# A long-convolution filter and a gated MLP on one core: the filter's sums and differences formed by TensorE, a third buffer for its values, and the second step's loads issued with the first

## The chip, the cores and the metric

One NeuronCore of a Trainium2 chip runs the kernel. The metric is the device time of one execution in microseconds (us). The engines are named as the profile names them: PE is TensorE (PEld its weight loads), DVE is VectorE, ACT is ScalarE, POOL is GpSimd, and SP issues the DMAs.

## The reference

Four batches of 12480 positions with 128 channels are convolved along the positions with a filter that a small network makes, gated, and sent through an MLP. Everything is float32.

```python
h_mlp  = np.maximum(pos_emb @ w1, 0.0) @ w2          # 12480x64 @ 64x64, @ 64x128
h_filt = h_mlp * np.exp(-0.01 * pos)[:, None]
u = x * v
y = irfft(rfft(u, n=2*S) * rfft(h_filt, n=2*S))[:, :S, :]
z = (x * y).reshape(B * S, D)                          # 49920 x 128
h = z @ moe_w_in                                       # 128 -> 2048
out = (h * np.cos(h)) @ moe_w_out                      # 2048 -> 128
```

## The kernel before, in words

**The convolution** is a Fourier transform in two steps, done as matmuls with tables of cosines and sines. A position is n = n1 * 120 + n2 with n1 below 104 and n2 below 120. The first step (`f1_units`, matmul on L402) works along n1 into 96 frequencies, the second (`f2_units`, L442) along n2; then comes the product with the filter's spectrum (`f2_product`, L458 to L461) and two steps back (`i1_units`, L466, and `i2_units`, L491). Of every two opposite n2 (n2 and 119 - n2) the kernel keeps a sum and a difference, so that the second step needs half the table for each.

**The filter** is made first. `filter_load` brings eleven pieces of `pos_emb`; `filter_scale` multiplies them on DVE by the decaying window (which commutes with the ReLU, being positive); `filter_turn` transposes them on PE; `filter_hidden` (L341 to L346) multiplies by `w1` and lets ACT write the ReLU into `aT`. Two positions lie on the partitions of one tile: 64 hidden values of an even n2 on the lower half and of the odd n2 after it on the upper half. `w1_sb` and `w2_sb` are therefore block-diagonal. `filter_out` (L348 to L361) takes a pair of n2 and the pair opposite to it: two matmuls of 256 columns give four positions, ACT copies two of them to `above`, and DVE makes one sum and one difference from PSUM and `above` (L359), straight into `ftile`. There are 30 such calls.

**The signal.** `u_units` loads x and v by groups of four n2 (two tiles of 208 KB; three buffers for x, two for v), multiplies the two halves (`u_multiply`, L390, each half on the engine that a small function names), and makes sums on POOL and differences on DVE (`u_sums`, L396). For batch 0 it runs beside the filter, as the generator `first_u`; the loops that make the filter call `next(first_u)` a written number of times: twice an iteration from the fifth on in the hidden layer, 40 times in all in the 30 calls of `filter_out`, and then once for every two units of the filter's first step.

**The order of all this is written out by hand.** The schedule is manual: each engine runs its instructions in the order in which the program records them, and SP issues the DMAs in that order too. A DMA that has to wait holds up what stands behind it in SP's order. The stages of the first 345 us are: the hidden layer; `filter_out` with the signal; the filter's first step (`f1_evict_filter`, L424 to L435, each unit on ACT or on DVE by a share of 0.53) with the rest of the signal; the end of that step beside `inverse_tables`, which makes ten tables with POOL's arithmetic and ACT's Sin (`Tables.sines`; the Sin of a table is recorded `lag` tables later); the first step for batch 0 beside the conversion of `moe_w_in` from float64; `f2_both_units`, in which the second step of the signal and that of the filter share the table `w` that DVE and ACT make (L289, L291); and the first step back.

In `f2_both_units` the filter's values of two frequencies go from PSUM to a tile `h` (ACT, L614), are stored to DRAM (`hd`, L616) for the other batches, and are used by the product. The pool has two buffers of each tile. `w` is stored to `wd`.

**The long part.** From about 345 us on, the MLP's 98 groups of rows are the main thread (16 pieces each: `moe_up` L725 with a range reduction on ACT, DVE and POOL, `moe_act` L739 and L741, `moe_down` L750), and the convolutions of the batches are a generator `conv` from which a piece is drawn whenever the main thread has gone as many steps as the last piece was worth. `forward_units` is the chain first step, second step, first step back; `f2_units` loads `w` and `h` two iterations ahead from `wd` and `hd` into three buffers each (L581, L583). `moe_store` (L759 to L777) transposes a finished group on PE, copies it to `ob` on ACT (L765) and issues its stores on SP (L773), all at one place of the order, halfway through the pieces of the next group.

Of the kernel before, what the change touches and what calls it, by code (L numbers as in the profile page):

```python
# [9 lines left out]
F32 = mybir.dt.float32  # L10
U32 = mybir.dt.uint32
AF = mybir.ActivationFunctionType
ALU = mybir.AluOpType
# [3 lines left out]
P = 128  # L17
# [13 lines left out]
def kernel(  # L31
# [46 lines left out]
    nc = tc.nc  # L78

    B, S, D = x.shape  # L80
    FO = pos_emb.shape[1]
    DFF = moe_w_in.shape[1]
    N1, N2 = 96, 120
# [167 lines left out]

    def inverse_tables(pool):

        t = Tables(pool, nc.gpsimd, 2)
        part = t.whole([P, 1], [[1, 1]], channel_multiplier=1, name="part")
        part4 = t.whole([P, 1], [[1, 1]], base=1, channel_multiplier=4, name="part4")
        step = t.whole([P, P], [[1, P]], name="step")
        mid = t.whole([P, P], [[1, P]], base=-MID, name="mid")
        cs, rows, tw_t = back_tables(pool)
        yield from t.sines(step, part, N2, [(cs[:, 0, 0:H + 1], 1), (cs[:, 1, 0:H + 1], 0)],  # L260
                           eighths=slice(0, H + 1, H))
        yield from t.sines(step[:, 1:H], part, N2,
                           [(cs[:, 0, H + 1:], 0), (cs[:, 1, H + 1:], 1)])
        yield from t.sines(step, part4, 4 * N1,
                           [(rows[:, i, :], q) for i, q in enumerate((0, 1, 2, 3))])
        yield from t.sines(mid, part4, TURN, [(tw_t[:, 0, :], 1), (tw_t[:, 1, :], 0)],
                           eighths=slice(H - 1, N2, H))
        t.finish(1)
        for kept, made in ((csd, cs), (rowsd, rows), (twd, tw_t)):
            nc.sync.dma_start(kept[:, :, :], made[:, :, :])  # L270

# [68 lines left out]

    def filter_hidden(bank, aT, i, peT, w1_sb):  # L341

        pa = bank()
        nc.tensor.matmul(pa[:, 0:ROWS * H], w1_sb[:, :], peT[:, :], start=True, stop=True)
        nc.scalar.activation(aT[:, 0:H, i * ROWS:(i + 1) * ROWS],
                             pa[:, 0:ROWS * H].rearrange("p (n a) -> p a n", a=H), AF.Relu)  # L346

    def filter_out(pool, bank, aT, slots, j, w2_sb):  # L348

        ps = bank()  # L350
        for i, jj in enumerate((j, H - 1 - j)):
            nc.tensor.matmul(ps[0:FR, i * 2 * D:(i + 1) * 2 * D], aT[:, jj, 0:FR],
                             w2_sb[:, :], start=True, stop=True)
        above = pool.tile([FR, 2, CB, 2], F32, name="above", bufs=2)
        pj = ps[0:FR, :].rearrange("p (n b i) -> p n b i", n=4, i=2)
        nc.scalar.copy(out=above[:, :, :, :], in_=pj[:, 2:4])
        a = H - 2 - 2 * j
        for place, op in ((a, ALU.add), (ODD + a, ALU.subtract)):
            nc.vector.tensor_tensor(  # L359
                slots[0:FR, :, place:place + 2, :].transpose([0, 2, 1, 3]),  # L360
                pj[:, 1::-1], above[:, :, :, :], op=op)  # L361

    def n2s(g):

# [229 lines left out]
    def f2_both_units(bank):  # L594

        with tc.tile_pool(name="both", bufs=2) as pool:
            ws = {}

            def before(j):
                ws[j] = pool.tile([KE, 2, N2], F32, name="w")  # L600
                for i in range(2):
                    make_w(ws[j][:, i, :], 2 * j + i, half=bank)
                nc.sync.dma_start(wd[j, :, :, :], ws[j][:, :, :])

            def mm(j, ps, i):
                if i == 0:
                    ps = bank(), bank()
                for filt in range(2):
                    f2_mm(ps[filt], ws[j], 2 * j, i, filt=filt == 1)
                return ps  # L610

            def after(j, ps):
                h = pool.tile([N2, 2, 2, D], F32, name="h")
                nc.scalar.activation(h[:, :, :, :].rearrange("p g r d -> p (g r d)"),  # L614
                                     ps[1][0:N2, :], AF.Copy, scale=1.0 / M)
                nc.sync.dma_start(hd[j, :, :, :, :], h[:, :, :, :])  # L616
                yield from f2_product(pool, ps[0], h, 2 * j)

            yield from units(N1 // 2, F2_STEPS, before, mm, after, 4, ahead=1)
# [69 lines left out]

    def forward_units(bank, back):  # L690

        yield from f1_units(bank, slots[0:R, :, :, :])
        yield from f2_units(bank)
        next(back)
        yield from i1_units(bank)

# [3 lines left out]
    def first_row(n):  # L700
        return min(R + (n - 1) * P, NROWS) if n else 0
# [54 lines left out]
        nc.scalar.copy(out=ot[:, 0:m], in_=accs.pop(n)[:, 0:m])  # L756
        return ot

    def moe_store(pool, n, ot):  # L759
        m = rows_of(n)  # L760
        pt = ps_h.tile([P, BANK], F32, name="ph")
        for i in range(G):
            transpose(pt[0:m, i * D:(i + 1) * D], ot[:, i * m:(i + 1) * m], ident)
        ob = pool.tile([P, 2, UA * D], F32, name="ob", bufs=1)
        nc.scalar.copy(out=ob[0:m, :, :].rearrange("p h n -> p (h n)"), in_=pt[0:m, :])  # L765
        row = first_row(n)
        while row < first_row(n + 1):
            b, g, n1 = row // R // NG, row // R % NG, row % R
            count = min(R - n1, first_row(n + 1) - row)
            first, _, second, _ = n2s(g)  # L770
            start = out[b * S + n1 * N2 + first, :]
            at = row - first_row(n)
            nc.sync.dma_start(  # L773
                bass.AP(tensor=start.tensor, offset=start.offset,
                        ap=[[N2 * D, count], [(second - first) * D, 2], [1, UA * D]]),
                ob[at:at + count, :, :])
            row += count  # L777

    with tc.manual_schedule():
        with tc.tile_pool(name="psum", bufs=8, space=PSUM) as psum, \  # L780
                ExitStack() as first:
            def bank():
                return psum.tile([P, BANK], F32, name="ps")
# [5 lines left out]
            aT = above.rearrange("p b j i -> p b (j i)")  # L789


            keep = first.enter_context(tc.tile_pool(name="keep", bufs=1, side="right"))
            w2_sb = keep.tile([P, 2 * D], F32, name="w2_sb")
            nc.gpsimd.memset(w2_sb[:, :], 0.0)
            with tc.tile_pool(name="layers", bufs=1, side="right") as pool:
                w1_sb = pool.tile([P, P], F32, name="w1_sb")
                nc.gpsimd.memset(w1_sb[:, :], 0.0)
# [1 line left out]
                for m in range(2):  # L799
                    nc.sync.dma_start(  # L800
                        w1_sb[m * FO:(m + 1) * FO, m * FO:(m + 1) * FO], w1[:, :])
                    nc.sync.dma_start(
                        w2_sb[m * FO:(m + 1) * FO, m * D:(m + 1) * D], w2[:, :])
                for i in range(1, NCH):
                    pes[i] = filter_load(pool, i)
                first_u = u_units(0, 3, slots[0:R, :, :, :],
                                  lambda j, half: nc.vector if half and j % 3 and j < 18
                                  else nc.gpsimd)
                next(first_u)
                ident = pool.tile([P, P], F32, name="ident")  # L810
                make_identity(nc, ident)
                window = filter_window(pool)
                nc.gpsimd.memset(aT[:, 0:H, NCH * ROWS:FR], 0.0)
                sines = forward_tables(pool)
                peTs = {}
# [14 lines left out]
            fpool = first.enter_context(tc.tile_pool(name="ftile", bufs=1, side="right"))  # L830
            ftile = fpool.tile([P, CB, N1 + KF, 2], F32, name="ftile")
            clear_gap(ftile[0:FR, :, :, :])
            with tc.tile_pool(name="out", bufs=1, side="right") as pool:
                for j in range(H // 2):
                    filter_out(pool, bank, aT, ftile, j, w2_sb)
                    for _ in range(1 + (j % 3 == 0)):
                        next(first_u)
            f1 = f1_units(bank, ftile[0:FR, :, :, :], 0.53, f1_evict_filter)
            for _ in first_u:
                for _ in range(2):  # L840
                    next(f1)
            with tc.tile_pool(name="tables", bufs=1) as pool:
                sines = inverse_tables(pool)
                for i, _ in enumerate(f1):
                    if i % 5 == 0:
                        next(sines, None)
                for _ in sines:
                    pass
# [60 lines left out]
            next(conv)  # L909
        moe_turn(mpool, 0)  # L910
        steps = [(n, c) for n in range(NALL) for c in range(NFC)]
        hidden, gates, ots = {}, {}, {}
        for i in range(len(steps) + LAG):
            if i < len(steps):
                n, c = steps[i]
# [12 lines left out]
            if i < len(steps):  # L928

                if c == (LAG - 1 if n else NFC - 2) and n + 1 < NALL:  # L930
                    moe_turn(mpool, n + 1)
                if c == NFC // 2 and n - 1 in ots:
                    moe_store(mpool, n - 1, ots.pop(n - 1))
            owed += 1.0
            while owed > 0.0:
                owed -= next(conv, owed)
        for n in sorted(ots):
            moe_store(mpool, n, ots[n])
# [1 line left out]
_INS = ['x', 'v', 'pos_emb', 'w1', 'w2', 'moe_w_in', 'moe_w_out']  # L940
_OUTS = [((49920, 128), 'float32')]
# [25 lines left out]
```

## Time and profile before

| | |
|---|---|
| median of three runs | 3795.7 us (3795.18 to 3796.21) |
| the profiled execution, its own time | 3799.85 us |
| its span, first to last instruction | 3798.0 us |
| mean granted clock of TensorE | 0.991 |
| busy: PE, DVE, POOL, ACT | 3709.6, 2769.4, 2592.8, 2520.0 us |
| DMA | 276 MB, 24.8% of 16 engines |
| 0 to 31.9 us | hidden layer of the filter |
| 31.9 to 64.9 us | `filter_out` beside the signal |
| 64.9 to 96.5 us | filter's first step beside the signal |
| 96.5 to 120.9 us | its end, beside the ten tables |
| 120.9 to 169.8 us | signal's first step, conversion of `moe_w_in` |
| 169.8 to 277.5 us | joint second step |
| 277.5 to 342.8 us | first step back, conversion of `moe_w_out` |
| 342.8 us to the end | MLP with the convolutions beside it |

The profile gives durations in us, for one of an instruction in ns where that is marked; a count after "x" says how many instructions a group holds. A float32 matmul shows as two PE instructions. "Idle before" names what ended an engine's rest. In the table of waits a line is: the waiting engine and line, what it waited for, the total, how often, the longest. A busy share is an average over the stretch; what counts is which engine ends last there.

### The profile page before, as it was taken

Reading aid. Unit: us, or ns where it says so; the run is one execution under the profiler, and the core shown is the slowest. Engines: PE = TensorE matmul, PEld = TensorE weight load, DVE = VectorE, ACT = ScalarE, POOL = GpSimd, SP = SyncE. Lnnn points to the kernel's source line nnn. Section 1 sums busy time; section 2 is a strip of 40 time slices with the busy share of each in tenths; the row PEclk is TensorE's granted clock in tenths of the full one; section 3 lists DMA queues with packets and bytes.
Section 4 is the critical chain, followed back from the end, with each engine's and each line's share of the span. In section 5 each row is a group of like instructions: output and inputs, shape, how many; then the busy total and the mean of one; then the engine's idle time right before and its main releaser. Section 6 shows DMA issues by size and latency. Waiting matters only on the chain.

```text
span 3798.0 us, 47246 instructions
## 1 busy us (share of the span) xinstructions
PE 3709.6 (98%) x13546; PEld 2114.1 (56%) x13546; DVE 2769.4 (73%) x5658; ACT 2520.0 (66%) x4683; POOL 2592.8 (68%) x2342
## 2 busy tenths in 40 slices
PE   7898999999999999999999999999999999999999
PEld 6777555645466555555565556555566544444444
DVE  7887887678876777778766886788765566666666
ACT  5756776756665557766655557666664677777777
POOL 7667886478854665588845664788644577777776
PEclk9899999999999999999999999999999999999999
DMA  6253551022201650122203540222105300000000
GB/s 165 70 177 96 148 152 54 12 76 78 73 27 49 178 172 24 36 76 75 63 16 102 175 129 12 61 78 73 48 12 159 95 17 23 17 17 23 17 21 15
DMA packets 209499, 276.14 MB, mean 73 GB/s; under 512 B 17111, under 2 KB 146535, under 8 KB 209111
## 3 DMA queue, kind: packets, MB, share of 16 engines
q1 hardware_dynamic: 209239, 273.12, 24.8%
q8 instruction: 109, 1.79, 0.2%
q14 instruction: 151, 1.24, 0.1%
HBM read 193.64 MB, written 79.42 MB: 72 GB/s over the span
## 4 chain that ended last, share of the span: by engine, by line
PE 81%; POOL 7%; DVE 4%; DMA 3%; ACT 3%; issue 2%; SPq 0%; POOLq 0%; ACTq 0%; DVEq 0%
PE ph L725 31%; PE acc L750 26%; PE cv L750 5%; PE cv L491 4%; PE cv L466 4%; POOL f L734 4%; PE cv L402 3%; PE cv L442 3%; PE ph L126 2%; DMA hd<-h 1%; PE ps L402 1%; DMA tm<-td 1%; ACT cs L739 1%; DVE k L731 1%; POOL tm L295 1%
## 5 line engine op out<-in xcount | busy, mean ns | idle before, releaser
L734 POOL TENSOR_TENSOR f<-a,k 128x512 f32<-128x512 f32 (+1 forms) x1568 | 1988.7, 1268 | 1062.3 <-DVE k L731 1060.2
L725 PE MATMUL ph<-at,w_in_sb 128*128 128x512 f32 (+1 forms) x3136 | 1601.5, 592 | 5.8 <-DVE gt L741 5.3
L728 ACT ACTIVATE a<-ph,quarter 128x512 f32<-128x512 f32 (+1 forms) x1568 | 1073.4, 685 | 764.8 <-PE ph L725 755.7
L750 PE MATMUL acc<-gt,w_out_sb 128*128 128x512 f32 (+1 forms) x2688 | 1375.2, 593 | 9.7 <-ACT ot L756 9.3
L741 DVE TENSOR_TENSOR gt<-ph,cs 128x512 f32<-128x512 f32 (+1 forms) x1568 | 1077.7, 687 | 319.3 <-ACT cs L739 291.8
L731 DVE TENSOR_SCALAR k<-a 128x512 f32<-128x512 f32 (+1 forms) x1568 | 770.0, 491 | 629.9 <-ACT a L728 608.4
L739 ACT ACTIVATE cs<-f 128x512 f32<-128x512 f32 (+1 forms) x1568 | 980.5, 625 | 334.7 <-POOL f L734 332.4
L750 PEld LDWEIGHTS acc<-gt,w_out_sb 128*128 128x128 f32 x2688 | 506.1, 189 | 663.6 <-issue 620.4
L725 PEld LDWEIGHTS ph<-at,w_in_sb 128*128 128x128 f32 x3136 | 554.5, 190 | 339.5 <-issue 266.8
L461 POOL TENSOR_TENSOR slots<-slots,t 120x256 f32<-120x256 f32 x384 | 311.9, 818 | 63.8 <-DVE t L460 26.9
L491 PEld LDWEIGHTS cv<-slots,tm 96*104 96x104 f32 x1920 | 241.2, 171 | 109.3 <-issue 79.3
L491 PE MATMUL cv<-slots,tm 96*104 96x128 f32 x1920 | 255.5, 275 | 9.1 <-DVE tm L291 4.9
L750 PE MATMUL cv<-gt,w_out_sb 128*128 128x512 f32 (+1 forms) x448 | 224.5, 583 | 0.7 <-DVE gt L741 0.7
L466 PEld LDWEIGHTS cv<-cs,slots 120*96 120x96 f32 x1536 | 176.7, 167 | 67.6 <-issue 65.7
L466 PE MATMUL cv<-cs,slots 120*96 120x120 f32 x1536 | 183.1, 266 | 0.0
L442 PE MATMUL cv<-slots,w 124*120 124x256 f32 x576 | 173.6, 381 | 7.0 <-DMA w<-wd 7.0
L442 PEld LDWEIGHTS cv<-slots,w 124*120 124x120 f32 x576 | 103.8, 184 | 131.0 <-issue 118.1
L402 PEld LDWEIGHTS cv<-c,slots 104*124 104x124 f32 x768 | 132.5, 192 | 71.2 <-issue 58.3
L402 PE MATMUL cv<-c,slots 104*124 104x192 f32 x768 | 151.2, 326 | 4.8 <-DVE gt L741 3.5
L750 PEld LDWEIGHTS cv<-gt,w_out_sb 128*128 128x128 f32 x448 | 84.9, 190 | 104.5 <-issue 99.5
L390 DVE TENSOR_TENSOR xt<-xt,vt 104x256 f32<-104x256 f32 x177 | 138.3, 789 | 0.1
L476 DVE TENSOR_TENSOR slots<-cv,other 96x240 f32<-96x240 f32 x384 | 133.7, 394 | 4.2 <-ACT other L474 4.2
(129 smaller groups left out, 2585.8 us busy)
## 6 DMA issues: line engine op xcount, KB each, us to landing
h<-hd SPq DMA_DIRECT2D x144, 240.0 KB
tm<-td SPq DMA_DIRECT2D x96, 312.0 KB
xt<-in_x_dram SPq DMA_DIRECT2D x120, 208.0 KB
vt<-in_v_dram SPq DMA_DIRECT2D x120, 208.0 KB
xs<-in_x_dram SPq DMA_DIRECT2D x120, 208.0 KB
zd<-zs SPq DMA_DIRECT2D x119, 208.0 KB
zb<-zd SPq DMA_DIRECT2D x96, 256.0 KB
w<-wd SPq DMA_DIRECT2D x144, 116.2 KB
```

The source lines that it names most:

```text
L402: nc.tensor.matmul(ps[0:KE, i * 2 * N1:(i + 1) * 2 * N1], u[:, b, 0:KE, i], c1[0:u.shape[0], :, :].rearrange("p r k -> p (r k)"), start=Tr ...
L442: nc.tensor.matmul(pi, w[:, i, :], parts[0:KE, :, k], start=True, stop=True)
L461: nc.gpsimd.tensor_tensor(y[:, r], y[:, r], t[:, r], op=op)
L466: nc.tensor.matmul(ps[0:N1, (i * 2 + r) * N2:(i * 2 + r + 1) * N2], parts[0:N2, r, :, b, i], cs[:, r, :], start=True, stop=True)
L491: nc.tensor.matmul(ps[0:R, i * D:(i + 1) * D], t[:, i, r, :], slots[0:N1, :, place, :], start=(r == 0), stop=(r == 1))
L725: nc.tensor.matmul(ph[:, 0:m], w_in_sb[:, c * P:(c + 1) * P], ats[n][:, 0:m], start=True, stop=True)
L728: nc.scalar.activation(a[:, 0:m], ph[:, 0:m], AF.Identity, bias=quarter[:, 0:1], scale=INV_TWO_PI)
L731: nc.vector.tensor_scalar(out=k[:, 0:m], in0=a[:, 0:m], scalar1=ROUND, scalar2=ROUND, op0=ALU.add, op1=ALU.subtract)
L734: nc.gpsimd.tensor_tensor(f[:, 0:m], a[:, 0:m], k[:, 0:m], op=ALU.subtract)
L739: nc.scalar.activation(cs[:, 0:m], f[:, 0:m], AF.Sin, scale=TWO_PI)
L741: nc.vector.tensor_tensor(gt[:, 0:m], ph[:, 0:m], cs[:, 0:m], op=ALU.mult)
L750: nc.tensor.matmul(accs[n][:, 0:m], w_out_sb[:, c, :], gt[:, 0:m], start=(c == 0), stop=(c == NFC - 1))
```

## The change

The diff makes these edits.

1. `filter_hidden` writes the ReLU with two ACT instructions of 64 partitions. The upper half is written in reversed order of pairs, so that slice j of `aT` holds a position on the lower half and the opposite position on the upper half. `w2_sb` becomes three blocks of 128 columns: `w2` over `w2`, `w2` over minus `w2`, minus `w2` over `w2`; the signs are made by four POOL multiplies behind the loads of `w2`. `filter_out` becomes 60 calls with two matmuls of 128 columns each, of which one gives the sum and one the difference; a copy from PSUM to `ftile` follows, by DVE in every fourth call and else by ACT. `next(first_u)` comes in four of six calls, 40 times as before. The tile `above` of this stage, its pool and the memset of `w2_sb` go.
2. The second half of each of batch 0's products goes to DVE for all 30 groups (before: for those with `j % 3` and `j < 18`). The share of the filter's first step that ACT takes goes from 0.53 to 0.56. The pool with `w2_sb` lies at the other side and is closed before the tables.
3. `inverse_tables` uses a lag of 4 instead of 2.
4. `h` in `f2_both_units` has three buffers.
5. `forward_units` starts `f2_units`, and with it the first two pairs of loads, ahead of the first step.
6. `moe_store` is split: `moe_back` (transposes and copy) stays where it was, the stores are issued two pieces later.

```diff
-        t = Tables(pool, nc.gpsimd, 2)
+        t = Tables(pool, nc.gpsimd, 4)
...
-        t.finish(1)
+        t.finish(len(t.waiting))
...
         nc.tensor.matmul(pa[:, 0:ROWS * H], w1_sb[:, :], peT[:, :], start=True, stop=True)
-        nc.scalar.activation(aT[:, 0:H, i * ROWS:(i + 1) * ROWS],
-                             pa[:, 0:ROWS * H].rearrange("p (n a) -> p a n", a=H), AF.Relu)
+        pj = pa[:, 0:ROWS * H].rearrange("p (n a) -> p a n", a=H)
+        to = aT[:, 0:H, i * ROWS:(i + 1) * ROWS]
+        nc.scalar.activation(to[0:FO], pj[0:FO], AF.Relu)
+        nc.scalar.activation(to[FO:P, ::-1, :], pj[FO:P], AF.Relu)
...
-        for i, jj in enumerate((j, H - 1 - j)):
-            nc.tensor.matmul(ps[0:FR, i * 2 * D:(i + 1) * 2 * D], aT[:, jj, 0:FR],
-                             w2_sb[:, :], start=True, stop=True)
-        above = pool.tile([FR, 2, CB, 2], F32, name="above", bufs=2)
-        pj = ps[0:FR, :].rearrange("p (n b i) -> p n b i", n=4, i=2)
-        nc.scalar.copy(out=above[:, :, :, :], in_=pj[:, 2:4])
-        a = H - 2 - 2 * j
-        for place, op in ((a, ALU.add), (ODD + a, ALU.subtract)):
-            nc.vector.tensor_tensor(
-                slots[0:FR, :, place:place + 2, :].transpose([0, 2, 1, 3]),
-                pj[:, 1::-1], above[:, :, :, :], op=op)
+        lower = 2 * j < H
+        for i, block in enumerate((0, 1 if lower else 2)):
+            nc.tensor.matmul(ps[0:FR, i * D:(i + 1) * D], aT[:, j, 0:FR], w2_sb[:, block, :],
+                             start=True, stop=True)
+        a = H - 1 - 2 * j if lower else 2 * j - H
+        to = f[0:FR, :, a:ODD + a + 1:ODD, :].transpose([0, 2, 1, 3])
+        (nc.vector.tensor_copy if j % 4 == 0 else nc.scalar.copy)(
+            out=to, in_=ps[0:FR, 0:2 * D].rearrange("p (s b i) -> p s b i", s=2, i=2))
...
-                h = pool.tile([N2, 2, 2, D], F32, name="h")
+                h = pool.tile([N2, 2, 2, D], F32, name="h", bufs=3)
...
+        f2 = f2_units(bank)
+        next(f2)
         yield from f1_units(bank, slots[0:R, :, :, :])
-        yield from f2_units(bank)
+        yield from f2
...
-                                  lambda j, half: nc.vector if half and j % 3 and j < 18
-                                  else nc.gpsimd)
+                                  lambda j, half: nc.vector if half else nc.gpsimd)
...
+                for block, signs in ((1, (1.0, -1.0)), (2, (-1.0, 1.0))):
+                    for m, sign in enumerate(signs):
+                        half = slice(m * FO, (m + 1) * FO)
+                        nc.gpsimd.tensor_scalar(
+                            out=w2_sb[half, block, :], in0=w2_sb[half, 0, :], scalar1=sign,
+                            scalar2=None, op0=ALU.mult)
...
-                for j in range(H // 2):
-                    filter_out(pool, bank, aT, ftile, j, w2_sb)
-                    for _ in range(1 + (j % 3 == 0)):
-                        next(first_u)
-            f1 = f1_units(bank, ftile[0:FR, :, :, :], 0.53, f1_evict_filter)
+            for j in range(H):
+                filter_out(bank, aT, ftile, j, w2_sb)
+                if j % 6 not in (1, 4):
+                    next(first_u)
+            f1 = f1_units(bank, ftile[0:FR, :, :, :], 0.56, f1_evict_filter)
...
                 if c == NFC // 2 and n - 1 in ots:
-                    moe_store(mpool, n - 1, ots.pop(n - 1))
+                    obs[n - 1] = moe_back(mpool, n - 1, ots.pop(n - 1))
+                if c == NFC // 2 + 2 and n - 1 in obs:
+                    moe_store(n - 1, obs.pop(n - 1))
```

## The prediction

> **What bounds the kernel now.** I read the page first, then the busy time by stage, then the waits, then the time-ordered views of the places where TensorE rests. The page and six stages ahead of the long part (columns after the length: PE, PEld, DVE, ACT, POOL, each with its count, then PE clock, DMA share, GB/s):
>
> ```profile
> PE 3709.6 (98%) x13546; PEld 2114.1 (56%) x13546; DVE 2769.4 (73%) x5658; ACT 2520.0 (66%) x4683; POOL 2592.8 (68%) x2342
> ...
> 31.90:64.85 32.95, 26.11 (x120) 19.49 (x121) 30.19 (x83) 11.05 (x30) 27.46 (x32) 0.97 0.58 172
> 64.85:96.45 31.60, 31.14 (x176) 30.85 (x176) 28.78 (x96) 22.60 (x100) 28.75 (x39) 0.93 0.51 154
> 96.45:120.90 24.45, 17.72 (x84) 16.41 (x84) 20.46 (x77) 16.26 (x71) 19.34 (x50) 0.86 0.06 16
> ...
> 169.80:277.50 107.70, 97.22 (x482) 75.09 (x482) 92.86 (x288) 54.81 (x146) 67.76 (x96) 0.97 0.57 167
> ```
>
> From 345 us on TensorE is the bound: it is 98 to 100% busy in nearly every stretch, so there only a pause of TensorE counts. Ahead of 345 us no engine is full for long. The filter's output (31.9 to 64.85) and its first step beside the signal's products (64.85 to 96.45) are VectorE's: 30.2 of 33.0 us and 28.8 of 31.6. The stage to 120.9 ends with ten tables made on GpSimd. The joint second step (169.8 to 277.5) is VectorE's again.
>
> The waits, longest first in total, name two that the change is about (total, times, longest, in us):
>
> ```profile
> ACT h L614 <- DMA hd<-h: 19.0, 19, 1.4
> ...
> DVE slots L458 <- ACT h L614: 7.7, 20, 0.7
> ...
> PE cv L442 <- DMA w<-wd: 7.0, 1, 7.0
> ```
>
> The last is the only long pause of TensorE in the bound part. In order of time (start, length):
>
> ```profile
> 758.96 0.60 PE L126 MATMUL ph<-ident,ot 128*128 128x128 f32 x4
> ...
> 760.42 1.17 SPq L773 DMA_DIRECT2D out_dram<-ob  x3
> 761.70 0.26 SPq L581 DMA_DIRECT2D w<-wd  x1
> ...
> 766.54 1.18 PE L442 MATMUL cv<-slots,w 124*120 124x256 f32 x2 [6.99 <-DMA w<-wd]
> ...
> 770.93 1.90 PE L725 MATMUL ph<-at,w_in_sb 128*128 128x512 f32 x2
> 772.63 1.05 PE L750 MATMUL acc<-gt,w_out_sb 128*128 128x512 f32 x2
> ```
>
> SP stood at a store of `ob` until ACT had made it; the second step's first `w` stood behind that store, was issued at 761.70 and landed at 766.5. TensorE rested 7.0 us, then took 1.90 us for a pair that takes 1.02 us later, until about 773.3.
>
> [...] the granted clock is 0.50 from 766 to 772 us after the 7.0 us rest. [...] here the VectorE product, 0.41 us undisturbed, ends 0.28 us after the GpSimd product.
>
> ```profile
> 54.40 0.91 POOL L390 TENSOR_TENSOR xt<-xt,vt 104x256 f32<-104x256 f32 x1
> ...
> 55.09 0.50 DVE L390 TENSOR_TENSOR xt<-xt,vt 104x256 f32<-104x256 f32 x1
> ```
>
> [...]
>
> **The change, part by part** (minus is a gain).
>
> *Filter's hidden layer, 0 to 31.9: +2.0.* ACT gets eleven more ReLUs of 64x480. Cost by width: 64x288 takes 0.39 and 64x384 0.47 us, so 64x480 about 0.54; an iteration then holds 0.56 + 1.1 us of ACT, beside spacings of 1.5 to 2.3 us between the transposes. Second, four small GpSimd multiplies that wait for the `w2` loads (issued at 1.87 and 3.14) stand ahead of the four iotas that VectorE's first table needs at 4.41. The landing isn't shown. The first `pe` load took 3.1 us from issue to use, so `w2` lands between 4.7 and 6.2; with four multiplies of some 0.3 us and the memset of 0.5 the tables start 2.5 to 4 us later. Cover: signal products can't start before `vt` lands at 20.1 anyway. If that covers all, 0; if none, +4.
>
> *Filter's output: -4.0.* VectorE loses 60 sums (21.5 us) and gets 15 copies at about 0.42 (64x288 takes 0.45), 6.3 us. ACT's 30 copies become 45 at 0.37, 16.6 us; their writes go in pieces of 8 bytes, which no row shows: at twice the price ACT has 33 us and the stage keeps its length. TensorE issues 240 instead of 120, of 128 columns; 120 columns cost 0.112 each in a stretch that TensorE sets:
>
> ```profile
> 277.87 22.13 PE ps L466 x198
> ```
>
> 240 x 0.112 = 26.9 us. The stage also carries 13.3 signal groups (40 units of three). [...] 13.3 x 2.2 = 29.3, now last. 33.0 becomes 29 (27 to 33).
>
> *First step beside the signal: +4.0.* All second halves of products now go to VectorE (`j % 3` and `j < 18` are gone). The f1 units there are 37. A VectorE unit takes 1.37 us:
>
> ```profile
> 97.25 0.45 DVE L429 COPY ftile<-ps 64x288 f32<-64x288 f32 x1
> ...
> 98.62 0.45 DVE L429 COPY ftile<-ps 64x288 f32<-64x288 f32 x1
> ```
>
> Share 0.53 to ACT becomes 0.56: VectorE has 16.1 units, 22.2 us, plus 12.3 groups at 0.50 (product) and 0.54 (difference)[...]: 12.8. Sum 35.0, and 0.6 of handovers: 35.6 for 31.6. [...]
>
> *Tables: 0.* A longer lag lets ACT off 6.2 us of waiting at 93.5 to 99.7. But GpSimd's ten tables fill 96.5 to 119.4 and their last Sin precedes ACT's last two units as before; that end is late next. 0, at best -3.
>
> *Third `h` buffer: -5.0.* A step of the joint stage holds two `w` at 0.59 together and four products spaced 0.35: 2.0 us of VectorE. Steps take (276.9 - 174.7)/48 = 2.13. ACT waits for a buffer that its store holds (3.1 to 4.0 us in the chain), and then VectorE for ACT. A buffer is held for 0.6 (made) + 0.4 (issue) + 4.0 = 5 us at most; two last 4 us of steps, three 6. 48 x 0.11 = 5; the 7.7 us that VectorE waited for ACT's `h` bound it above at 7, and nothing is gained if VectorE's work alone sets the step. VectorE stays the bound.
>
> *Second step's loads ahead of the first: -10.4.* Rest 7.0, and half of the 6.8 us at half clock, 3.4. The instruction order has `w`, `h`, `w`, `h` ahead of the four stores that stood before them; the first step, 64 units, lies between issue and use, and the third pair's store is moved behind it too. The loads must wait until the signal group's buffers are read; SP then holds stores and `zb` for a few us, needed later. The other two transitions show no wait. Without the gain 0.
>
> *Store split in two: -1.0.* SP stops less ahead of `tm` loads, which TensorE awaited for 2.6 us in all; ACT and TensorE keep their order. 0 to -2.6.
>
> Sum: 2.0 - 4.0 + 4.0 + 0 - 5.0 - 10.4 - 1.0 = **-14.4 us**. The profiled execution took 3799.85 (span 3798.0), so it would be 3785.4. The median of the runs is 3795.7, 4.15 lower; I keep the difference: **3781.3**.
>
> **Rivals.** A measurement tells 0.2%, 7.6 us, from no change.
> - *The filter gains more.* [...] +1, -5, 0, third buffer -5.6, rest as above: -21, **3774.7**. For: VectorE holds 10 us less there before the groups. Against: 35 us of work counted for one stage.
> - *VectorE fuller than counted.* +3, -3, +6, buffer -1: -6.4, **3789.3**. For: VectorE is busy 92.9 of the joint stage's 107.7 us already, its start included.
> - *The loads are hidden but TensorE waits there for something else* (the evictions, which ended at 755.5, speak against): -4.0, **3791.7**.
> - [...]
> That TensorE really forms the sums is settled by the instruction order (120 matmuls of 128 columns, no sums left).
>
> **How the numbers follow.** Forecast 0.45 (alone 3776 to 3788), more gain 0.25, fuller VectorE 0.15, other wait 0.10[...]. Range 3773 to 3792[...]. Faster: 0.45 + 0.25 + a third of 0.15 + a little = 0.76; slower 0.06; same 0.18.
>
> **What would show it.** Right: no wait of TensorE on `w`, clock 1.00 around 760; `h` no longer waiting on `hd`, joint stage near 102 us; the output stage near 29 us with VectorE near 20; the next near 36 with VectorE full and products above 0.41. Wrong: TensorE resting at that transition; a filter part that ends under 118 or over 127 us; a stall in the long part that was not there.

## The result and the profile after

| | before | after |
|---|---|---|
| median beside each other | 3795.51 us (4 runs) | 3789.41 us (4 runs) |
| ratio, with its 95% interval | | 0.9984 (0.9967 to 1.0001) |
| median, repeated later with more runs | 3795.86 us (47 runs) | 3788.32 us (18 runs) |
| ratio, repeated | | 0.9981 (0.9975 to 0.9988) |
| the profiled execution, its own time | 3799.85 us | 3790.69 us |
| its span | 3798.0 us | 3788.8 us |

The change gains 6 to 7.5 us, just under the 0.2% (7.6 us) that the prediction called the bound of what can be told. The repetition's interval leaves out a ratio of 1, so there is a gain. The forecast was 3781.3, so half of the 14.4 us foreseen didn't come. One execution alone says little here: the 47 runs of the kernel before reach from 3791.2 to 3800.4 us.

The stages ahead of the long part, in the view of busy time by stretch (start and end, length, then PE, PEld, DVE, ACT, POOL with counts, granted clock, DMA share, GB/s), for the changed kernel:

```profile
36.10:63.20 27.10, 26.41 (x240) 26.25 (x241) 16.07 (x40) 17.11 (x45) 23.36 (x25) 1.00 0.63 185
63.20:99.70 36.50, 33.43 (x188) 30.29 (x188) 33.48 (x104) 27.13 (x120) 24.27 (x29) 1.00 0.49 145
99.70:124.20 24.50, 13.58 (x69) 12.69 (x69) 17.95 (x69) 13.94 (x61) 19.35 (x50) 0.88 0.06 16
...
173.70:276.80 103.10, 97.30 (x480) 75.27 (x480) 92.60 (x287) 58.53 (x142) 67.21 (x96) 0.96 0.59 173
```

The first line is the filter's output: shorter by 5.9 us than before, and now TensorE's (26.41 of 27.10 us, 240 instructions for 120 matmuls), no longer VectorE's (16.07). The second is the filter's first step beside the signal: longer by 4.9 us, VectorE and TensorE both 33.4 of 36.5. The third, the tables, has its length of before. The last is the joint second step, shorter by 4.6 us in this view; from the stage's first matmul to the first of the step back it is 3.3 (106.3 us before, 103.1 now).

The first stretch has grown from 31.9 to 36.1 us. The time-ordered view of GpSimd and VectorE (start, length, what ended the idle time before):

```profile
3.99 0.77 POOL L819 TENSOR_SCALAR w_sb<-w_sb 64x128 f32<-64x128 f32 x1 [1.96 <-DMA w_sb<-in_w_dram]
5.40 1.70 POOL L819 TENSOR_SCALAR w_sb<-w_sb 64x128 f32<-64x128 f32 x3 [0.63 <-DMA w_sb<-in_w_dram]
7.78 0.15 DVE L237 TENSOR_SCALAR quarter_p<-part 128x1 f32<-128x1 f32 x1 [3.41 <-POOL part L190]
...
25.00 0.42 DVE L390 TENSOR_TENSOR xt<-xt,vt 104x256 f32<-104x256 f32 x1
25.56 1.58 POOL L396 TENSOR_TENSOR slots<-xt 104x256 f32<-104x256 f32 x1 [5.51 <-DVE xt L390]
```

The four sign multiplies wait for the `w2` loads and hold GpSimd to 7.1 us; VectorE's first table operation starts at 7.78 instead of 4.41. Its later scales and table steps are about 3 us late too. The second half of the first group's product now stands behind them, is made at 25.00, and GpSimd rests 5.5 us until then.

At the transition near 760 us TensorE no longer rests. The first two loads of `w` were issued at 617.61 and 618.31 and the third at 719.65, all ahead of the store at 758.11:

```profile
617.61 0.26 SPq L581 DMA_DIRECT2D w<-wd  x1
...
719.65 0.33 SPq L581 DMA_DIRECT2D w<-wd  x1
...
756.64 0.60 PE L126 MATMUL ph<-ident,ot 128*128 128x128 f32 x4
757.08 0.60 PE L442 MATMUL cv<-slots,w 124*120 124x256 f32 x2
758.11 1.18 SPq L778 DMA_DIRECT2D out_dram<-ob  x3
```

The second step's matmul follows the transposes without a pause. Later there is a stall that the execution before did not have:

```profile
1395.33 0.78 SPq L778 DMA_DIRECT2D out_dram<-ob  x2
1396.15 0.42 SPq L711 DMA_DIRECT2D zb<-zd  x1
...
1397.46 0.32 SPq L660 DMA_DIRECT2D tm<-td  x1
...
1404.14 1.11 PE L491 MATMUL cv<-slots,tm 96*104 96x128 f32 x8 [1.91 <-DMA tm<-td]
1405.09 1.84 PE L727 MATMUL ph<-at,w_in_sb 128*128 128x512 f32 x2
```

Stores, `zb` and `tm` go out within 2.1 us of each other (before, the stores were issued at 1401.20 and `zb` at 1408.52). `tm` comes late, TensorE rests 1.91 us and then runs at half clock (1.84 us for a pair that takes 1.02). Lining up the 1568 gate multiplies of both executions (L741 before, L743 after, one for each piece of the long part) shows what each place is worth: the changed kernel is 2.3 us ahead when the long part begins, 12.6 after the transition at 760, 13.2 just before 1404 and 9.4 after the stall, which so cost 3.8; it ends 9.2 ahead.

### The profile page after: what moved, and what is told of

The parts are those of the page before. It is cut to its first block, busy times and chain, and to the rows that moved or that the text cites. A ratio compares the mean times of both kernels' runs of the same rounds, so it can differ in the third digit from the quotient of the medians.

```text
span 3788.8 us, 47457 instructions
## 1 busy us (share of the span) xinstructions
PE 3705.8 (98%) x13666; PEld 2114.8 (56%) x13666; DVE 2761.4 (73%) x5621; ACT 2539.4 (67%) x4719; POOL 2585.1 (68%) x2327
## 3 DMA queue, kind: packets, MB, share of 16 engines
q1 hardware_dynamic: 209239, 273.12, 24.3%
## 4 chain that ended last, share of the span: by engine, by line
PE 83%; POOL 7%; DVE 3%; ACT 2%; issue 2%; DMA 2%; SPq 0%; POOLq 0%; DVEq 0%; ACTq 0%
PE ph L727 31%; PE acc L752 27%; PE cv L752 5%; PE cv L491 4%; PE cv L466 4%; POOL f L736 4%; PE cv L402 3%; PE cv L442 3%; PE ph L126 2%; PE ps L442 1%; PE ps L402 1%; POOL tm L295 1%; ACT cs L741 1%; DMA tm<-td 1%; DVE k L733 1%
## 5 line engine op out<-in xcount | busy, mean ns | idle before, releaser
L743 DVE TENSOR_TENSOR gt<-ph,cs 128x512 f32<-128x512 f32 (+1 forms) x1568 | 1077.9, 687 | 319.4 <-ACT cs L741 292.0
L741 ACT ACTIVATE cs<-f 128x512 f32<-128x512 f32 (+1 forms) x1568 | 980.4, 625 | 338.7 <-POOL f L736 335.8
L390 DVE TENSOR_TENSOR xt<-xt,vt 104x256 f32<-104x256 f32 x195 | 146.2, 756 | 5.4 <-DMA vt<-in_v_dram 4.9
```

Of the source, the lines that this page charges most:

```text
L741: nc.scalar.activation(cs[:, 0:m], f[:, 0:m], AF.Sin, scale=TWO_PI)
L743: nc.vector.tensor_tensor(gt[:, 0:m], ph[:, 0:m], cs[:, 0:m], op=ALU.mult)
```

## The experiments

All differ from the changed kernel or from the kernel before by the lines shown. The ratio in brackets is to the kernel before, run on the same chip; where two experiments were not run together, it is the ratios that compare.

**The store split undone in the changed kernel.**

```diff
                 if c == NFC // 2 and n - 1 in ots:
-                    obs[n - 1] = moe_back(mpool, n - 1, ots.pop(n - 1))
-                if c == NFC // 2 + 2 and n - 1 in obs:
-                    moe_store(n - 1, obs.pop(n - 1))
+                    moe_store(n - 1, moe_back(mpool, n - 1, ots.pop(n - 1)))
```

> The changed kernel with one edit undone: a tile's stores are issued together with its transposes and copy, two steps earlier than in the changed kernel. Theory one (the split store lies beside the loads of zb and tm, so TensorE waits 1.9 us for tm near 1404 us and then runs at half clock): the wait and the half clock go, about 3.4 us less, so 3786 us against 3789.4. Rival (the wait for tm is set by how this tile's loads happen to meet other transfers, and any shift moves it): a wait of 1 to 2 us for tm stands at some tile all the same, and the time stays at 3788.5 to 3790.5 us.

Measured: 3788.57 us (0.9979, 0.9970 to 0.9988). In its trace no wait near 1404 us is left: TensorE's wait for `tm` is 1.9 us in all instead of 5.0. But the time is that of the changed kernel, as the rival says. Its reason doesn't follow from this: the longest wait for `tm` that is left, 1.2 us at 438 us, stands in the kernel before too (0.95 us) and was not moved there. The stall is real in the trace and small in the median.

**The changed kernel once more.**

> The changed kernel once more, unaltered, beside the others on one chip, for a median of as many runs as theirs. If the wait of 1.9 us for tm near 1404 us with its half clock belongs to this kernel, its profile shows it again and the time is 1 to 3 us above that of the kernel with the stores together (3788.6). If that wait is an accident of one execution, it stands elsewhere or nowhere, and the time is 3788.5 to 3789.5 us.

Measured: 3788.32 us (0.9981, 0.9975 to 0.9988). The wait near 1404 us is there again, but of 0.98 us, and the clock stays at 1.00. So the wait is there, as the first text says, but the time is not above that of the kernel with the stores together. By the same alignment, between 1395 and 1430 us, the eight traces with the split (this one and those of experiments below among them) lose 3.8 us in the first profile of the changed kernel and 0.6 to 1.2 in the seven others, this one 1.2. The five without it, other than the kernel before, lose nothing there. So in the traces the split costs about 1 us at this place, which the medians can't tell (3788.32 against 3788.57); the rest of the 3.8 us in the first profile was one execution's longer wait and half clock.

**The early loads alone, in the kernel before.**

```diff
+        f2 = f2_units(bank)
+        next(f2)
         yield from f1_units(bank, slots[0:R, :, :, :])
-        yield from f2_units(bank)
+        yield from f2
```

> The kernel before with one edit alone: the second step's first loads are issued with the first's. Theory one (the wait for w near 760 us and the half clock behind it cost about 10 us, and nothing downstream gives it back): 3785.5 us, that is 10 below the kernel before, and below the whole change. Rival (what is won near 760 us is lost again at a later wait, such as that for tm): 3789 to 3793 us, and the alignment of the long part's products falls back after 760 us.

Measured: 3787.88 us (0.9976, 0.9968 to 0.9985). This one edit gives 8.8 us against its own kernel before (3796.72), as much as the whole change. Nothing is given back.

**The late loads, in the changed kernel** (the same lines undone).

> The changed kernel with the loads of the second step put back behind the first. Theory one: the wait of TensorE for w near 760 us returns with its half clock, about 10 us more: 3799.5 us, slower than the kernel before by some 4. Rival (the other edits share in the gain, so that the wait is shorter here than before): 3792 to 3796 us.

Measured: 3789.80 us (0.9983, 0.9976 to 0.9990): neither the theory nor the rival. The wait for `w` had not returned at all. SP's order in this kernel tells why:

```profile
720.09 0.28 SPq L581 DMA_DIRECT2D w<-wd  x1
720.43 0.41 SPq L583 DMA_DIRECT2D h<-hd  x1
...
758.51 1.19 SPq L776 DMA_DIRECT2D out_dram<-ob  x3
```

The `w` loads are recorded after the first step again, and go out 102 us later than in the changed kernel, but still 38 us ahead of the store, which is early enough. What had held them before was not their own place but the store recorded ahead of them, at which SP stood from 721.9 to 760.4 us (in that profile SP's wait for ACT's `ob` at L773 lasted 38.4 us). The split puts the stores two pieces later, behind `w`. So two of the edits remove the same wait, each alone. Two more kernels test this.

**Both undone in the changed kernel** (the diffs of the first and of this last).

> The changed kernel with two edits undone: the second step's loads behind the first step again, and a tile's stores issued together with its transposes and copy. With the loads alone put back (3789.8 us) TensorE's wait for w had not returned. New theory (the wait near 760 us comes from the stores: SP holds w's load behind a store of ob that is recorded ahead of it and waits for its copy; stores that are issued two pieces later stand behind w's load instead, so either edit alone removes the wait): with both undone the wait returns, about 7 us with 3 us of half clock, and the time is near 3799 us. Rival (the wait went with the change of phase that any edit brings): no wait, 3788.5 to 3790.5 us.

Measured: 3796.61 us (1.0003, 0.9995 to 1.0011). The wait is back (in its trace SP, then TensorE):

```profile
758.80 1.17 SPq L776 DMA_DIRECT2D out_dram<-ob  x3
760.08 0.26 SPq L581 DMA_DIRECT2D w<-wd  x1
```

```profile
764.57 1.18 PE L442 MATMUL cv<-slots,w 124*120 124x256 f32 x2 [6.64 <-DMA w<-wd]
765.55 1.91 PE L725 MATMUL ph<-at,w_in_sb 128*128 128x512 f32 x2
```

Everything else in the change together (filter, `h` buffer, tables) is worth nothing: 3796.6 against 3795.9. The pair of edits is worth 3796.61 - 3788.32 = 8.3 us.

**The split alone, in the kernel before.**

```diff
-                    moe_store(mpool, n - 1, ots.pop(n - 1))
+                    obs[n - 1] = moe_back(mpool, n - 1, ots.pop(n - 1))
+                if c == NFC // 2 + 2 and n - 1 in obs:
+                    moe_store(n - 1, obs.pop(n - 1))
```

> The kernel before with one edit alone: a tile's stores are issued two pieces after its transposes and copy; the second step's loads stay behind the first. New theory (SP's order of ob's store and w's load is all that matters): the wait for w is gone, about 3787.5 to 3788.5 us, like the loads' edit alone (3787.9). Rival (the other edits were needed): the wait stands, 3796 us or, with waits for tm moved, up to 3799.

Measured: 3789.01 us (0.9983, 0.9975 to 0.9991), and no wait for `w`. 6.9 us from the edit that the prediction priced at 1.0.

**Two `h` buffers in the changed kernel.**

```diff
-                h = pool.tile([N2, 2, 2, D], F32, name="h", bufs=3)
+                h = pool.tile([N2, 2, 2, D], F32, name="h")
```

> The changed kernel with two buffers for the filter's values again. Theory one (the third buffer took the wait of VectorE's products for ScalarE's copy out of the joint step): the joint stretch grows from 103.1 to about 106.4 us, 2.13 us a step, and the time is 3.3 us more, about 3792.7 us. Rival (the shorter step came from the other edits, or its gain is given back at the end of the stretch and at the restart of the long part): 3789 to 3790 us.

Measured: 3793.02 us (0.9990, 0.9983 to 0.9996), 4.7 above the changed kernel's repetition, or 3.4 by the ratios (0.9990 - 0.9981 = 0.0009 of 3796). The wait that the third buffer removed is back in the table of waits, with nearly the amount of before (7.7 us there); a step takes 2.12 us again, and the stretch from the first matmul to the first of the step back 105.4 us against 102.9 in the repetition:

```profile
DVE slots L458 <- ACT h L614: 7.3, 21, 0.7
```

**The signs later, in the changed kernel.**

```diff
-                for block, signs in ((1, (1.0, -1.0)), (2, (-1.0, 1.0))):
...
                     next(sines, None)
+                    if i == 0:
+                        for block, signs in ((1, (1.0, -1.0)), (2, (-1.0, 1.0))):
...
```

> The changed kernel with its four sign multiplies moved behind the iotas of the first tables, so that VectorE's first table no longer waits for the loads of w2. Theory one (the 3.4 us by which the tables start late are the 4.2 us by which the hidden layer ends late): the hidden layer ends at 32 to 33 us instead of 36.1, the time falls by 3.5 to 4 us to about 3785.5. Rival (the end of the hidden layer is set by the second half of the first group's product, which now stands in VectorE's order behind a scale of the filter, so that GpSimd and what follows wait for it anyhow): the layer ends at 35 to 36 us and the time stays within 1 us of the changed kernel's.

Measured: 3787.34 us (0.9978, 0.9970 to 0.9985), 1.0 below the repetition; the intervals overlap. In the trace the tables start at 4.43 and the hidden layer ends at 33.4 us instead of 36.7, so theory one holds for the stage. At 334.7 us TensorE is still 3.8 us ahead, but the first gate multiply is only 1.4 ahead: this execution's half clock at the start of the long part lasted 13.7 us, the repetition's 6.8. The 1.0 us in the median is too small to be told from what such a difference between executions makes.

**The old sharing of the products, in the changed kernel**, alone and with the signs later.

```diff
-                                  lambda j, half: nc.vector if half else nc.gpsimd)
+                                  lambda j, half: nc.vector if half and j % 3 and j < 18
+                                  else nc.gpsimd)
```

> The changed kernel with batch 0's products shared between the engines as before (the second half on VectorE only for two of three of the first 18 groups, else on GpSimd). Theory one (the 4.9 us by which the filter's first step beside the signal got longer are VectorE's added products): that stretch goes from 36.5 back to about 32 us, the filter's output stays near 27 us since TensorE sets it, and the time falls from 3788.3 to about 3783.5 us. Rival (GpSimd, with 9 us more in that stretch and 3 us more in the one before, becomes last in both): the two stretches together lose 2 us at most, 3786.5 to 3788.5 us.

Measured: 3785.53 us (0.9977, 0.9966 to 0.9988), 2.8 below the changed kernel (1.5 by the ratios), between the two texts. Busy time of the filter's output and of the stretch after it, in this kernel:

```profile
36.20:65.30 29.10, 27.06 (x240) 26.29 (x240) 14.69 (x36) 17.19 (x45) 24.25 (x28) 1.00 0.57 167
65.30:99.30 34.00, 31.44 (x176) 28.32 (x176) 29.61 (x92) 26.55 (x118) 30.84 (x41) 1.00 0.53 154
```

Each second stretch is taken to the end of the last signal sum, 99.3 us here and 99.7 in the changed kernel's first profile (100.7 in its repetition). In it VectorE gives up 3.9 us (33.5 to 29.6) and GpSimd takes 6.6 more (24.3 to 30.8), and it is shorter by 2.5 us, not 4.9; the first stretch is longer by 2.0. Together they take 63.1 us against 63.6 (64.0 in the repetition), as the rival says. TensorE, GpSimd and VectorE are now all at 30 to 31 us of 34: no engine has the room to take the products. The gain in time is not clear of the noise, as the intervals of the two kernels overlap.

> The changed kernel with both repairs: the sign multiplies behind the first iotas, and the products shared as before. If the two add, with 1.0 us of time and 3.2 us in the trace for the first and 4.8 us expected of the second, the filter's three stages end 8 us earlier and the time is 3780 to 3782.5 us, below the kernel before by some 14. If the end of the three stages is held by something that neither touches (the loads of x and v), they add to 4 us or less, 3784 us or more.

Measured: 3784.99 us (0.9972, 0.9962 to 0.9982): the rival's number. GpSimd's last signal sum, behind which its tables stand, ends at 97.2 us against 100.7, 3.5 earlier, not 8; in the kernel before it was 96.4. The two repairs bring the new filter about back to where the old one was. Whether the loads hold the stages, as the rival's text has it, or the engines' shares do, this run doesn't separate.

**The buffer and the early loads alone, in the kernel before.** The tile with `w2` is closed before the tables as in the changed kernel: without that the third buffer finds no room.

```diff
-                h = pool.tile([N2, 2, 2, D], F32, name="h")
+                h = pool.tile([N2, 2, 2, D], F32, name="h", bufs=3)
...
+        f2 = f2_units(bank)
+        next(f2)
         yield from f1_units(bank, slots[0:R, :, :, :])
-        yield from f2_units(bank)
+        yield from f2
```

> The kernel before with only the third buffer for the filter's values and the second step's loads ahead of the first (the tile with w2 is closed before the tables, as in the changed kernel, to make room for the buffer). If the new filter costs about 5 us in the end, as the changed kernel with both transition edits undone says (3796.6 us with the buffer's gain of 4.7 in it, against 3795.9), then this one lies 4 to 5 us below the loads alone (3787.9) and below the whole change: 3783 to 3784 us. Rival (the buffer needs the changed filter to gain, or gives its gain back at the end of the joint stretch): 3787 to 3788.5 us.

Measured: 3782.86 us (0.9967, 0.9954 to 0.9979), as expected, and 5.5 below the changed kernel (5.3 by the ratios): the price of the new filter with its tables, and of the split.

**TensorE kept busy before the long part**, on top of the last kernel. Nothing reads what the 14 added matmuls make.

```diff
             beside(i1_units(bank), [(w_out_sb[:, c, :], w) for c, w in out_pieces], some_groups)
+            fill = bank()
+            for _ in range(14):
+                nc.tensor.matmul(fill[0:N1, 0:2 * N1], c1[0:R, 0, :],
+                                 c1[0:R, :, :].rearrange("p r k -> p (r k)"),
+                                 start=True, stop=True)
```

> The kernel with the third buffer and the early loads alone, and 14 matmuls of a table with itself, whose result nothing reads, put where TensorE rests 4.9 us before the long part (338 to 343 us in the kernel before). Theory (the half clock after that rest, seen for 5 to 11 us in the traces, costs half of its length, so part of the executions' spread and 2.5 to 5.5 us of each comes from it): TensorE's rest shrinks below 1.5 us, the clock stays at 1.00 from 338 us on, and the time is 3778 to 3780.5 us against 3782.9, with less spread. Rival (TensorE isn't the last engine there, or the added matmuls push the start of the long part back): 3782 to 3785 us.

Measured: 3778.74 us (0.9955, 0.9941 to 0.9968), the fastest of all. Busy time around the restart, first without and then with the added matmuls:

```profile
342.00:346.00 4.00, 3.40 (x15) 2.73 (x14) 0.69 (x1) 0.71 (x2) 0.62 (x1) 0.50 0.77 224
346.00:350.00 4.00, 4.00 (x16) 2.93 (x15) 0.40 (x2) 1.27 (x3) 1.06 (x1) 0.68 0.24 64
```

```profile
342.00:346.00 4.00, 3.41 (x25) 2.76 (x26) 1.09 (x3) 2.36 (x6) 1.25 (x2) 1.00 0.67 180
346.00:350.00 4.00, 2.12 (x11) 1.13 (x10) 2.01 (x5) 2.48 (x6) 2.54 (x3) 1.00 0.57 166
```

The clock stays at 1.00 through the restart. The profiled execution (3783.38) had a wait of 1.88 us for `tm` at 349.7 and 3.4 us of half clock behind it; the other four took 3778.05 to 3779.80. Five runs are few, but four of them lie below every one of the five of the kernel without the fill (3780.77 to 3784.47). The two kernels ran on different chips, and the intervals of their ratios overlap, so the gain in time isn't settled. In the traces it is plain: from the end of the step back to the first gate multiply pass 17.0 us without the fill and 13.4 with it.

## Why the prediction was right, and where not

The side was right and the time within the range; the size was half of the forecast. Predicted and measured, in us:

| step of the prediction | predicted | profile | runs |
|---|---|---|---|
| hidden layer | +2.0 | +4.2 | |
| filter's output | -4.0 | -5.9 | |
| first step beside the signal | +4.0 | +4.9 | |
| tables | 0 | 0 | |
| these together | +2.0 | +3.2 | +4 to +5 |
| third `h` buffer | -5.0 | -3.3 | -3.4 to -4.7 |
| start of the long part (not in the prediction) | | -2.3 | |
| loads ahead and store split | -11.4 | -10.2, +3.8 | -8.3 |
| sum | -14.4 | -9.2 (whole span) | -7.5 |

**The filter and the transition share the miss**, with 2 to 3 us each; the buffer adds 0.3 to 1.6. The filter's +4 to +5 is the 5.5 us between the changed kernel and the one without the new filter and the split, less about 1 for the split; the same follows from the kernel with both of the transition's edits undone, which lies 0.8 above the kernel before although it has the buffer's gain of 3.4 to 4.7 in it. In the hidden layer the prediction named the mechanism, gave 0 to +4 and chose the middle. The tables' delay of 2.5 to 4 us came out at 3.4, but by luck: the `w2` loads landed earlier than estimated (the first multiply began at 3.99), and the four multiplies took 2.5 us instead of 1.2. The cover that it named failed: `vt` landed at 19.0 us and the signal's products waited for it, but it isn't they that end the layer. The filter's scales on VectorE do, and they stand behind the table steps that the signs delay. Moving the signs gave 3.3 us of stage length in one pair of kernels (36.7 to 33.4) and 1.2 in the other (36.2 to 35.1), so they are part of the 4.2 and not surely all. The filter's output gained more than forecast: its signal groups took about 2.1 us each, not 2.2 (the author's estimate from 0.73 us twice on GpSimd and 0.41 and 0.43 on VectorE, taken as if hardly any of it overlapped), and TensorE's 26.4 us of matmuls, which the prediction had as 26.9 in second place, end last. These were 26.1 us before, with half as many matmuls of twice the width, so the sums cost TensorE almost nothing. The doubt about ACT's writes in pieces of 8 bytes did not come true: its 45 copies took 17.1 us, 0.38 each.

The next stage grew by 4.9 for the forecast +4.0, but the account of it was too simple. The prediction took it for VectorE's, with 28.8 of 31.6 us; its own line has TensorE at 31.1, partly at half clock (mean 0.93). With the old sharing of the products the stage was 2.5 us shorter, so the products explain half of the 4.9; the other 2.4 are not explained by any run. In all, TensorE took over sums in a stage in which it was already needed for 26 of 33 us, so 6 us could be had; the products that VectorE got saved 2.0 us there and cost 2.5 in the next stage, where TensorE and VectorE stand at 33 of 36.5 us. Stage lengths account for 3.2 us. In the repetition the changed kernel is behind the kernel without the new filter by 3.5 us at the last signal sum, 4.2 when the joint step begins, 4.4 when it ends and 5.1 at 338 us, the end of the step back. The new share of 0.56 and the longer lag were not run alone; ACT still waited 5.0 us for the first table, of the 6.2 that the lag was to take away.

**The third buffer was near in size, and right for VectorE**: VectorE's wait for ACT's `h` (7.7 us before) is gone, and it came back with two buffers. But the sign that the prediction gave, `h` no longer waiting on `hd`, did not come. ACT's wait for a store to free a buffer was 19.0 us in 19 times before, and is now:

```profile
ACT h L614 <- DMA hd<-h: 22.9, 28, 1.4
```

It no longer reaches VectorE. By the ratios 3.4 us in the changed kernel and as much in the kernel before (0.9976 to 0.9967), by the medians 4.7 and 5.0. The step went from 2.13 to 2.03 us. The profile's -3.3 is lower since the end of the stretch, from the last `h` to the first matmul of the step back, grew from 2.3 to 3.6 us.

**The transition was right in its wait and wrong in its cause.** The prediction read that `w` stood behind a store of `ob`, and then priced only the edit that issues the loads earlier. Under the store split it wrote that SP stops less ahead of `tm`, -1.0, and that ACT and TensorE keep their order; it did not ask which DMAs the stores are moved behind. They are moved behind the same `w` loads. The split alone gives 6.9 us, the loads alone 8.8, both together 8.3: the two overlap and must not be added. The split's own side effect is near +1 us in the traces, where -1.0 stood; in the profiled execution it was +3.8, for the longer wait and the half clock that followed there, so that the prediction's own sign of being wrong, a stall in the long part that was not there, did come. The 10.4 us for wait and clock were right for the profiled execution: by the alignment the place cost 10.2 us in the kernel before, and 9.5 in the kernel with both edits undone, where half clock lasted 6.8 us instead of 10.2. Part of either spell falls into the pause itself, so the difference is small. The 8.3 us between the medians fit these less the split's 1.

**The offset between executions.** The prediction kept the 4.15 us by which the profiled execution lay above its median. After the change the profiled one lay 1.3 us above its own. Part of the difference is the start of the long part: in both profiles the step back ends at 338 us, yet the changed kernel's first gate multiply is 2.3 us earlier, since its half clock there lasted 6.8 us and not 13.7.

Of the rivals, "VectorE fuller than counted" gave 3789.3, which is the time measured, but by other terms: its buffer gain of -1 was wrong, and its +6 for the stage beside the signal was no nearer to the measured +4.9 than the forecast's +4; the number agrees by chance. The 0.05 for a slower kernel stood for 3804.8 us, if VectorE's operations with two inputs had to wait for GpSimd's; that was the author's estimate, and it did not decide: over these two stages the median of VectorE's products went from 0.46 to 0.43 us and that of its differences stayed at 0.43; GpSimd's products grew from 0.73 to 0.95. The two lines of the prediction leave it open whether one waits for the other, since the VectorE product ends 0.28 us after GpSimd's, less than its own 0.41.

## What to carry to other kernels

Where a queue stands at an instruction that waits, ask of every edit which moves anything in that queue whether it lets the same victim pass: two edits that free one load are worth one of them (here 6.9 and 8.8 us alone, 8.3 together). Before work is moved from the engine that ends a stage, add up the other engines' time in that stage and in the next; the gain is only the distance to the second. And in these runs a pause of TensorE cost its own length (7.0 us at 760) and about half of the half clock in which it then worked (1.90 us for a pair that takes 1.02), so a pause of known length that can't be removed may be worth filling.

## What the runs showed of the hardware

The spells of half clock had lengths in steps. They were 3.4 us (among others after the two waits of 1.9 us), 6.8 (at the start of the long part in eight of the profiled executions, and after the wait of 6.6), 10.2 (after the wait of 7.0 in the kernel before) and 13.7 (at the start of the long part in the kernel before and in four others): one to four times 3.4 us. They are counted from where the clock falls, often still in the pause: in the kernel before at 762.4, where TensorE works again from 766.5.

The length of the pause alone doesn't set the length of the spell: at the start of the long part spells of 6.8 and 13.7 us follow a pause of the same 4.9 us. In the eight short spells TensorE was busy for 9 to 38% of the first 3.4 us of half clock, in the five long ones for 0 to 3%. Why that goes with 6.8 or with 13.7 us isn't shown. The price of the spell is: from the end of the step back to the first gate multiply pass 14.4 to 14.8 us in the eight, 16.9 to 17.0 in the five and 13.4 with the fill. So this one place makes 2.1 to 2.6 us between two executions, about a quarter of the spread of 9 us among the runs of the kernel before.

The clock also falls after shorter rests than those of 4.9 to 7.0 us. Both profiles, of the kernel before and of the changed kernel, run at half clock for 3.4 us near 391 and near 511 us too (from 393.8 and 513.3 us in the first, from 391.4 and 510.9 in the second). In the kernel before TensorE rests 1.5 and 0.6 us shortly before the first of these falls (busy time by stretch, before and behind the fall):

```profile
390.39:393.80 3.41, 1.39 (x3) 0.57 (x4) 2.92 (x5) 2.52 (x5) 2.71 (x3) 1.00 0.59 196
393.80:397.21 3.41, 3.41 (x11) 2.35 (x11) 2.54 (x6) 1.62 (x4) 2.63 (x3) 0.50 0.21 59
```

TensorE was busy for 41% of the 3.41 us before that fall. In these two profiles all eight falls between 339 and 1406 us follow 3.41 us in which it was busy for 16 to 45%. Laid off in steps of 3.41 us from one change of the clock to the next, the other stretches at full clock in the long part, up to 8 us before the end (about 1000 in an execution), have it busy for 57% or more; two profiles don't make a rule of it. Each of the two places near 391 and 511 us costs TensorE about 2.1 us of rest and, by half of the 3.4 us, an estimated 1.7 us of slower work; no edit here went after them.
